# Seven products of half matrices in a float32 output projection on one Trainium2 core

## The chip, the cores and the metric

The kernel runs on one core of one Trainium2 chip. The metric is device time in microseconds (us), as the median of several runs. The engines are named as in the profile: PE is TensorE (matmuls), PEld its weight loads, DVE is VectorE, ACT is ScalarE, POOL is GpSimd, SP is SyncE, which here only issues DMAs. "SP's queue", "ACT's queue" and "POOL's queue" are the DMAs that an engine issues, in its program order: a DMA that has to wait holds up those behind it, and the engine's own work too.

## What is computed

The kernel mixes an attention block A and a block of product-key experts B with a gate per token. S = 2048 tokens, D = 1024, 32 heads of 32.

```python
def _A_ref(x, wqkv, wo):
    ...
    p = _softmax(scores, axis=-1)
    o = jnp.einsum("bhqk,bhkd->bhqd", p, v)
    return (lambda x, *d: x.transpose(*d))(o, 0, 2, 1, 3).reshape(B, S, D) @ wo

def _B_ref(x, w_q, k1, k2, u, v):
    ...
    act = _gelu(jnp.einsum("nd,nhkd->nhk", xf, ue))
    out = jnp.einsum("nhk,nhk,nhkd->nd", g, act, ve)
    return out.reshape(B, S, D)

x = A_x
g = _sigmoid((x * gate_w).sum(-1, keepdims=True))
a = _A_ref(x, A_wqkv, A_wo)
b = _B_ref(x, B_w_q, B_k1, B_k2, B_u, B_v)
return g * a + (1 - g) * b
```

The change concerns the last product, `o @ wo` (2048 x 1024 by 1024 x 1024), and what is added to it from B: a 2048 x 64 matrix of weights (with 1 - g in it) times the 64 x 1024 table v.

## The kernel before

Large products are made in float32r: an operand x is split into hi (x copied to float32r by ACT) and lo (x - hi, by DVE), and hi·hi + hi·lo + lo·hi is summed in PSUM, three matmuls for one. A matmul multiplies 128 x 128 weights into 128 x 512 moving elements, which fill one bank of PSUM. The function `split` (lines 88 to 90) issues one ACT and one DVE instruction.

The order is written out by hand: each engine runs its instructions in the order of the program. The stages, in this order:

- Q and K for all heads, from x and wqkv (line 325); the keys' fold; then the router (line 401 and its helpers).
- The values' stage: V for 16 tiles of 128 tokens, in two halves of 512 columns (`values`, line 566). A tile has 24 matmuls. `values_out` copies a bank to SBUF on ACT (line 569) and stores it by ACT's queue. The banks come from a ring of 8 in the pool `ps1`. The last tile of the second half, tile 15, uses a bank of the pool `pso`, which takes the place of bank 7 when `ps1` is closed; bank 7 was last used by tile 14. Within this stage the experts' weights are turned (`peer_turn`, lines 611 to 620) and stored to DRAM as `ATD`, through a tile `at` with one buffer.
- The 32 heads: scores (line 725), exp on ACT (735), the product with V (746) and sums of rows. `finish` stores a head's unscaled output to DRAM (`OD`); `norm_sums` stores its sums (`SMD`), `load_r` and `norm_r` make reciprocals for four heads and store them (`RD`). Meanwhile wo (`wo_raw`, 16 pieces of 256 KB), v and AT are loaded for the last stage, each at a step of its own.
- The output projection: 8 chunks of 256 tokens (W = 256). A chunk is loaded transposed by `load_chunk(n, k0, k1)` on SP's queue (8 loads of `OD` into a buffer named V, and 4 of the reciprocals, each row to 32 partitions, into rb0 or a buffer named accd), for chunk 1 on POOL's queue. Chunk 0 comes in eighths kc = 0 to 7 as wo is split (`split_hi`, `split_lo`); the last eighth, kc = 7, needs the sums of head 31, made right at the start of this stage: sums to `SMD` (smd<-ssb), back (rr<-smd), reciprocal, to `RD` (rd<-rr), back for each chunk (rb<-rd, accd<-rd). The chunks 1 to 7 are scaled and split by `split_o` one chunk ahead. `wo_mm` makes the 4 banks of a chunk (2 blocks of 128 tokens by 2 halves of 512 columns), 24 matmuls each; `av_mm` adds two matmuls of the experts to each bank. `store` copies a chunk's banks by ACT and DVE in turn and stores them by SP's queue.

Of the kernel before, what the change touches and what calls it, by code (L numbers as in the profile page):

```python
# [9 lines left out]
F32 = mybir.dt.float32  # L10
# [6 lines left out]
S = 2048  # L17
# [13 lines left out]
def gated_mha_peer_kernel(ctx, tc, xT, wqkv, wv, wo, wq, k12, ug, v, out):  # L31
# [537 lines left out]
    def values_out(ts, ps, half, copy=lambda o, p: nc.scalar.activation(o, p, AF.Copy)):  # L569
# [75 lines left out]
    load_shift(0, Z)  # L645
    values_out(*fin0)
    values_out(*values(list(range(4)), 1))
    for t in range(4, NT - 1):
        values_out(*values([t], 1))

    ps1.close()
    pso = Pool("pso", space=PSUM, side="right")

    values_out(*values([NT - 1], 1, lambda: pso.tile([128, 512], F32, name="o")),
               nc.vector.tensor_copy)
    vw.close()
    sm2.close()
    sm.close()
# [3 lines left out]


    keep = Pool("keep")
    wo_raw = keep.tile([128, KC, D], F32, name="wo_raw")
    v_raw = keep.tile([128, D], F32, name="v_raw")
    AT = keep.tile([128, S], F32R, name="AT")
    rb0 = keep.tile([128, KC, W], F32, name="rb0")
    wk = Pool("wk", bufs=2)
    vpool = Pool("vpool", bufs=2)  # L670
    kq = Pool("kq")
# [162 lines left out]
    def split_first(step):  # L834
        o = OC[0][:, 0, :]
        if step == 0:
            W0.append(zp.tile([128, 2, D], F32R, name="z1"))
            OH[0] = zp.tile([128, KC, W], F32R, name="z0")
            OL[0] = wk.tile([128, KC, W], F32R, name="acc")
            nc.vector.tensor_mul(o, o, RB[0][:, 0, :])  # L840
        elif step == 1:
            nc.scalar.activation(W0[0][:, 0], wo_raw[:, 0, :], AF.Copy)
        elif step == 2:
            nc.scalar.activation(OH[0][:, 0, :], o, AF.Copy)
        else:
            for lo, src, hi in ((W0[0][:, 1], wo_raw[:, 0, :], W0[0][:, 0]),
                                (OL[0][:, 0, :], o, OH[0][:, 0, :])):
                nc.vector.tensor_tensor(out=lo, in0=src, in1=hi.bitcast(F32), op=OP.subtract)

# [2 lines left out]
    def at(step, f, *a):  # L852
        todo.setdefault(step, []).append((f, a))
# [16 lines left out]
        at((H - 1) * NT + step, split_first, i)  # L870
    at((H - 1) * NT + 13, merge, H - 1)
    for k in range(2 * KC):
        c = slice(k * D // 2, (k + 1) * D // 2)
        at((8 + k) * NT + 11, dma, wo_raw.rearrange("p k m -> p (k m)")[:, c], wo[:, c])
    for i in range(2):
        at(28 * NT + 6 + i, dma, v_raw[64 * i:64 * i + 64, :], v)
        at(28 * NT + 13 + 10 * i, dma, AT[:, i * S // 2:(i + 1) * S // 2],
           ATD[:, i * S // 2:(i + 1) * S // 2])
# [24 lines left out]
    kq.close()  # L903


    fin = Pool("fin")
    ps_even = Pool("ps_even", space=PSUM)

# [6 lines left out]
    def split_o(n, k0, k1):  # L915

        if k0 == 0:
            OH[n] = zp.tile([128, KC, W], F32R, name=f"z{n % 2}")
            OL[n] = wk.tile([128, KC, W], F32R, name="acc")
        o = OC[n][:, k0:k1, :]  # L920
        nc.vector.tensor_mul(o, o, RB[n][:, k0:k1, :])
        split(OH[n][:, k0:k1, :], OL[n][:, k0:k1, :], o)

    def wo_mm(pa, n, kcs, first, last):
        for kc in kcs:
            wh, wl = (W0[0][:, 0], W0[0][:, 1]) if n == kc == 0 else (woh[kc], wol[kc])
            for a, b, i in ((OH[n], wh, 0), (OH[n], wl, 1), (OL[n], wh, 2)):
                for tt, half in pa:
                    nc.tensor.matmul(pa[tt, half], a[:, kc, tt * 128:(tt + 1) * 128],  # L929
                                     b[:, half * 512:(half + 1) * 512],  # L930
                                     start=(first and kc == kcs[0] and i == 0),
                                     stop=(last and kc == kcs[-1] and i == 2))

    def av_mm(pa, n):
        for (tt, half), ps in pa.items():
            tok = slice(n * W + tt * 128, n * W + (tt + 1) * 128)
            for b in (vh, vl):
                nc.tensor.matmul(ps, AT[:, tok], b[:, half * 512:(half + 1) * 512],  # L938
                                 start=False, stop=False)

    def banks(n):
        pool = (ps_even, ps_odd)[n % 2]
        return {(tt, half): pool.tile([128, 512], F32, name=f"pa{tt}{half}")
                for tt in range(W // 128) for half in range(2)}

    def store(pa, n, pieces=1):
        m = 512 // pieces
        for (tt, half), ps in pa.items():
            r = fin.tile([128, 512], F32, name="res", bufs=3)
            for i in range(pieces):  # L950
                c = slice(i * m, (i + 1) * m)
                if (half + i) % 2:
                    nc.scalar.activation(r[:, c], ps[:, c], AF.Copy)
                else:
                    nc.vector.tensor_copy(r[:, c], ps[:, c])
                dma(out[n * W + tt * 128:n * W + (tt + 1) * 128,
                        half * 512 + i * m:half * 512 + (i + 1) * m], r[:, c])


    def split_hi(kc):  # L960
        nc.scalar.activation(woh[kc], wo_raw[:, kc, :], AF.Copy)
        if kc < KC - 1:
            o = OC[0][:, kc, :]
            nc.vector.tensor_mul(o, o, RB[0][:, kc, :])
            nc.scalar.activation(OH[0][:, kc, :], o, AF.Copy)

    def split_lo(kc):
        nc.vector.tensor_tensor(out=wol[kc], in0=wo_raw[:, kc, :],
                                in1=woh[kc].bitcast(F32), op=OP.subtract)
        if kc < KC - 1:  # L970
            nc.vector.tensor_tensor(out=OL[0][:, kc, :], in0=OC[0][:, kc, :],
                                    in1=OH[0][:, kc, :].bitcast(F32), op=OP.subtract)

    ps_odd = None
    pa = banks(0)
    wo_mm(pa, 0, [0], True, False)
# [3 lines left out]
    load_chunk(1, 0, KC - 1, nc.gpsimd)  # L980
    split_hi(1)
# [12 lines left out]
    split(woh[0], wol[0], wo_raw[:, 0, :])  # L994
    ps_odd = Pool("ps_odd", space=PSUM)
    vhl = fin.tile([128, 2, D], F32R, name="vhl")
    vh, vl = vhl[:, 0], vhl[:, 1]
    split(vh, vl, v_raw)
    av_mm(pa, 0)
    split_lo(KC - 1)  # L1000
    split_o(0, KC - 1, KC)
    wo_mm(pa, 0, [KC - 1], False, True)
    for k0, k1 in ((0, KC // 2), (KC // 2, KC)):
        split_o(1, k0, k1)
    load_chunk(2, 0, KC)
    NW = S // W
    for n in range(NW - 2):
        nxt = banks(n + 1)
        wo_mm(nxt, n + 1, list(range(KC - 1)), True, False)
        av_mm(nxt, n + 1)  # L1010
        split_o(n + 2, 0, KC)
        if n + 3 < NW:
            load_chunk(n + 3, 0, KC)
        store(pa, n)
        wo_mm(nxt, n + 1, [KC - 1], False, True)
        pa = nxt

    n = NW - 1
    for k, (key, ps) in enumerate(banks(n).items()):
        one = {key: ps}  # L1020
        wo_mm(one, n, list(range(KC - 1)), True, False)
        av_mm(one, n)
        if k == 0:
            store(pa, n - 1)
        wo_mm(one, n, [KC - 1], False, True)
        store(one, n, 2)
    ps_odd.close()
    ps_even.close()
    fin.close()
# [32 lines left out]
```

## Time and profile before

| what | us |
|---|---|
| median of 3 runs | 1886.46 (1884.76 to 1887.77) |
| profiled execution, its own time | 1886.32 |
| its span, first to last instruction | 1884.6 |
| matmul of wo, 128x512: busy / weight load | 0.389 / 0.188 |
| copy of a 128x512 bank: ACT / DVE | 0.60 / 0.68 |
| subtraction on DVE: 128x256 / 512 / 1024 / 2048 | 0.42 / 0.69 / 1.22 / 2.29 |
| values' stage, matmuls from 480.7 to 658.1 | 177 |
| heads, from 658.2 to 1688.7 | 1031 |
| output projection, from 1688.7 to the end | 196 |

The span is what the profile's instructions cover; the execution's own time has 1.7 us around it. The granted clock of TensorE is 0.998 on the mean. In the page, a share is of the span. The chain of waits follows the execution back from its last instruction: at each step it goes to what released that instruction, so an engine with a large share there sets the time. In the timelines a line reads: start, length, engine and line of the kernel, operation, out<-in, shapes, and in brackets the idle time before it and what ended it. Matmuls overlap: a busy time of 0.389 us stands for one that starts every 0.227 us. In the values' stage between 480 and 652 us DVE is busy for 32.2 us and ACT for 30.2 us of 172; the DMA engines are used to 24%.

### The profile page before, as it was taken

The numbers are of one execution on the slowest core, as the hardware profiler recorded it, in microseconds if no ns is written. First come the engines' busy times: TensorE is split into PE (matmuls) and PEld (weight loads), VectorE is DVE, ScalarE is ACT, GpSimd is POOL, SyncE is SP. The second block draws the span as 40 slices with busy tenths as digits, with TensorE's granted clock in tenths as the row PEclk, the third lists the DMA queues.
The fourth block names the chain that finished last, engine by engine and source line by source line (L and its number), as shares of the span: only waits on it lengthen the run. The fifth ranks groups of instructions, "written<-read, shape, count | busy, mean of one in ns | idle before, by whom it ended". The sixth has DMA issues, their size and how long they took to land.

```text
span 1884.6 us, 25741 instructions
## 1 busy us (share of the span) xinstructions
PE 1874.6 (99%) x10271; PEld 1157.2 (61%) x10271; DVE 1203.3 (64%) x917; ACT 1158.3 (61%) x1412; POOL 148.6 (8%) x183
## 2 busy tenths in 40 slices
PE   9999999999999999999999999999999999999999
PEld 7877777887888844444444444444444444448887
DVE  4522224877520078888888888888888888895220
ACT  4211111200121199999999999999999999993110
POOL 0000000035200000000000000000000000010000
PEclk9999999999999999999999999999999999999999
DMA  5777774420222177777777777777687777756521
GB/s 212 279 265 254 266 275 137 136 77 5 79 95 80 45 178 159 168 167 162 166 172 179 169 181 169 184 166 181 158 187 162 172 166 177 189 128 167 155 90 67
DMA packets 108082, 302.72 MB, mean 161 GB/s; under 512 B 14724, under 2 KB 48660, under 8 KB 84472
## 3 DMA queue, kind: packets, MB, share of 16 engines
q1 hardware_dynamic: 70520, 154.76, 27.3%
q0 software_dynamic: 14976, 103.29, 26.4%
q10 hardware_dynamic: 22464, 43.00, 7.1%
q8 instruction: 81, 1.33, 0.3%
q14 instruction: 41, 0.34, 0.1%
HBM read 138.73 MB, written 62.66 MB: 107 GB/s over the span
## 4 chain that ended last, share of the span: by engine, by line
PE 99%; ACT 0%; DMA 0%; DVE 0%; issue 0%; ACTq 0%; DVEq 0%
PE ring L725 28%; PE o L746 25%; PE bk L325 16%; PE pa L929 9%; PE bk L566 9%; PE bk L401 5%; PE bk L211 2%; PE bk L272 2%; PE ring L759 1%; PE pa L938 1%; PE o L566 0%; DMA w0raw<-in_wqkv 0%; PE bk L286 0%; PE o L759 0%; ACT P L735 0%
## 5 line engine op out<-in xcount | busy, mean ns | idle before, releaser
L735 ACT ACTIVATE P<-ring 128x512 f32<-128x512 f32 (+2 forms) x1034 | 914.5, 984 | 22.2 <-PE ring L725 8.2
L774 DVE TENSOR_TENSOR acc<-acc,P 128x2048 f32<-128x2048 f32 x319 | 731.0, 2291 | 76.3 <-ACT P L735 50.0
L746 PE MATMUL o<-P,V 128*32 128x512 f32 x3840 | 465.4, 599 | 0.0
L725 PE MATMUL ring<-z,z 98*128 98x512 f32 x1024 | 273.0, 408 | 1.4 <-ACT P L735 1.1
L725 PE MATMUL ring<-Q,K 98*128 98x512 f32 x1024 | 272.0, 407 | 0.2 <-ACT P L735 0.2
L725 PEld LDWEIGHTS ring<-z,z 98*128 98x128 f32 x1024 | 182.6, 188 | 144.4 <-ACT P L735 75.4
L725 PEld LDWEIGHTS ring<-Q,K 98*128 98x128 f32 x1024 | 182.0, 188 | 144.3 <-ACT P L735 72.7
L746 PEld LDWEIGHTS o<-P,V 128*32 128x32 f32 x3840 | 98.8, 109 | 223.5 <-issue 214.7
L89 ACT ACTIVATE hi<-bk 128x512 fp32r<-128x512 f32 x64 | 37.6, 598 | 242.8 <-PE bk L325 226.4
L325 PE MATMUL bk<-xh,whi 128*128 128x512 f32 x448 | 176.2, 393 | 0.1
L325 PE MATMUL bk<-xh,wlo 128*128 128x512 f32 x448 | 174.4, 389 | 0.0
L325 PE MATMUL bk<-xl,whi 128*128 128x512 f32 x448 | 174.4, 389 | 0.0
L768 POOL DMA_DIRECT2D accd<-P x95 | 81.5, 858 | 1100.4 <-ACT P L735 368.6
L90 DVE TENSOR_TENSOR lo<-bk,hi 128x512 fp32r<-128x512 f32 x64 | 44.2, 690 | 188.1 <-ACT hi L89 183.9
L772 DVE TENSOR_TENSOR acc<-P 128x2048 f32<-128x2048 f32 x32 | 73.4, 2292 | 74.3 <-ACT P L735 74.3
L325 PEld LDWEIGHTS bk<-xh,whi 128*128 128x128 f32 x448 | 84.1, 188 | 24.0 <-issue 6.7
L566 PE MATMUL bk<-wvh,xh 128*128 128x512 f32 x248 | 96.7, 390 | 0.0
L566 PE MATMUL bk<-wvh,xl 128*128 128x512 f32 x248 | 96.5, 389 | 0.0
L566 PE MATMUL bk<-wvl,xh 128*128 128x512 f32 x248 | 96.5, 389 | 0.0
L325 PEld LDWEIGHTS bk<-xh,wlo 128*128 128x128 f32 x448 | 84.1, 188 | 17.8
L325 PEld LDWEIGHTS bk<-xl,whi 128*128 128x128 f32 x448 | 84.1, 188 | 17.0
L569 ACT ACTIVATE vo<-bk 128x512 f32<-128x512 f32 x31 | 18.5, 597 | 109.3 <-PE bk L566 103.4
(163 smaller groups left out, 1660.7 us busy)
## 6 DMA issues: line engine op xcount, KB each, us to landing
accd<-P POOLq DMA_DIRECT2D x95, 1024.0 KB, 7.5
wqt<-in_wq SPq DMA_DIRECT2D x32, 1024.0 KB
vd<-vo ACTq DMA_DIRECT2D x32, 256.0 KB
z<-kdh SPq DMA_DIRECT2D x32, 256.0 KB
z<-qdh SPq DMA_DIRECT2D x32, 256.0 KB
V<-vd SPq DMA_DIRECT2D x32, 256.0 KB
K<-kdh SPq DMA_DIRECT2D x32, 256.0 KB
Q<-qdh SPq DMA_DIRECT2D x32, 256.0 KB
```

Source lines behind the costliest of these rows:

```text
L90: (on or nc.vector).tensor_tensor(out=lo, in0=src, in1=hi.bitcast(F32), op=OP.subtract)
L211: nc.tensor.matmul(b0[w, n], w0[w][a][:, kc, :], b[:, kc, n * 512:(n + 1) * 512], start=(kc == 0 and i == 0), stop=(kc == KC - 1 and i == 2))
L325: nc.tensor.matmul(ps, a[:, kc, :], b[:, kc, n * 512:(n + 1) * 512], start=first, stop=last)
L401: nc.tensor.matmul(ps, a[:, kc, tok], b, start=first, stop=last)
L566: nc.tensor.matmul(p, a[:, kc, tok], b, start=first, stop=last)
L725: on_ring(nc.tensor.matmul(ring[:, i, :], K[:98, kt * 128:(kt + 1) * 128], Q[:98, qc * 512:(qc + 1) * 512], start=True, stop=True), i)
L735: on_ring(nc.scalar.activation(P[h, kt][:, q0 * 512:(q0 + m) * 512].rearrange("p (a m) -> p a m", a=m), ring[:, i:i + m, :], AF.Exp, scale ...
L746: nc.tensor.matmul(O[h][32 * qc:32 * qc + 32, :], Vt[g][:, kt, 32 * j:32 * j + 32], p[:, qc * 512:(qc + 1) * 512], start=(kt == 0), stop=( ...
L768: nc.gpsimd.dma_start(ACCD[h], P[h, kt], accum_op=OP.add)
L772: nc.vector.tensor_add(ACC[h], P[h, 0], P[h, kt])
L774: nc.vector.tensor_add(ACC[h], ACC[h], P[h, kt])
L929: nc.tensor.matmul(pa[tt, half], a[:, kc, tt * 128:(tt + 1) * 128], b[:, half * 512:(half + 1) * 512], start=(first and kc == kcs[0] and i ...
```

## The change

A product of 2 x 2 half matrices can be made with seven products of halves (in the Winograd form) in place of eight. For the chunks 1 to 7, A is the chunk's 256 tokens x 1024 and B is wo; A11 is the first 128 tokens by the first 512 of the inner dimension, A12 those tokens by the other 512, and B11 the first 512 rows by the first 512 columns. The combinations are S1 = A21 + A22, S2 = S1 - A11, S3 = A11 - A21, S4 = A12 - S2 and T1 = B12 - B11, T2 = B22 - T1, T3 = B22 - B12, T4 = B21 - T2, and each product is split into hi and lo as before. A chunk is one `unit`: the products A11·B11, S3·T3, S1·T1, S2·T2, A12·B21, S4·B22, A22·T4 (12 matmuls each), the experts' matmuls (two for each of the four results, one result in a bank of its own), and sums of the banks on DVE. In a unit the next chunk is scaled, combined and split (`ahead`); the places of the operands have one buffer each, freed by the product that reads them. Chunk 0 is made as before, but the first product of chunk 1 is put ahead of its last eighth.

The combinations T1 to T4 don't depend on the chunk. They are made in the values' stage, in four groups i = 0 to 3 (`load_early`, `split_early`), and stored to DRAM (`TD`); a fifth group does v (`VPD`). The loads of group i stand behind `values_out` of tile 4 + 2i, the subtractions and splits behind that of tile 5 + 2i. In the last stage `load_t` loads them (2 loads of 1 MB each for T1 to T3, 8 of 256 KB for T4), partly over buffers of wo that are done with. AT is loaded by chunk. `norm_r` and the loads of the last eighth move from inside the loop over kc to behind it.

The core of the diff:

```diff
+    TD = [[dram.tile([128, KC // 2, 512], F32R, name=f"t{i}{part}") for part in "hl"] for i in range(4)]
+    VPD = [dram.tile([128, D], F32R, name=f"vp{part}") for part in "hl"]
...
     values_out(*values(list(range(4)), 1))
+    th = Pool("th", bufs=2)
+    raw = {}
+
+    def load_early(i):
+        for j in range(4 if i < KC // 2 else 2):
+            raw[j] = wvp.tile([128, 512], F32, name="wvraw")
+            if i < KC // 2:
+                c0 = (i + j // 2 * KC // 2) * D + j % 2 * 512
+                dma(raw[j], wo[:, c0:c0 + 512])
+            else:
+                for k in range(2):
+                    dma(raw[j][64 * k:64 * k + 64, :], v[:, j * 512:(j + 1) * 512])
+
+    def split_early(i):
...
+        def parts(t, dst_hi, dst_lo):
+            hi, lo = th.tile([128, 512], F32R, name="th"), t.bitcast(F32R)
+            split(hi, lo, t)
+            dma(dst_hi, hi)
+            dma(dst_lo, lo)
+
+        if i < KC // 2:
+            b11, b12, b21, b22 = (raw[j] for j in range(4))
+            sub(b11, b12, b11)
+            sub(b12, b22, b12)
+            sub(b22, b22, b11)
+            sub(b21, b21, b22)
+            for k, t in enumerate((b11, b22, b12, b21)):
+                parts(t, *(d[:, i, :] for d in TD[k]))
+        else:
+            for j in range(2):
+                parts(raw[j], *(d[:, j * 512:(j + 1) * 512] for d in VPD))
+
     for t in range(4, NT - 1):
         values_out(*values([t], 1))
+        (load_early, split_early)[t % 2](t // 2 - 2) if t < NT - 2 else None
...
+    def product(a, b, *av):
+        ps = bank()
+        if av:
+            av_mm(*av, ps, first=True)
+        for k in range(HC):
+            for i, j in ((0, 0), (0, 1), (1, 0)):
+                nc.tensor.matmul(ps, AP[a][i][:, k, :], BP[b][j][k],
+                                 start=(not av and k == 0 and i == j == 0),
+                                 stop=(k == HC - 1 and i == 1))
+        return ps
...
     load_chunk(1, 0, KC - 1, nc.gpsimd)
+    for n in range(2):
+        load_at(n)
+    load_t(2, [zp.tile([128, S], F32R, name="z1")], [fin.tile([128, S], F32R, name="t3l")])
...
         if kc == 4:
-            norm_r(G - 1)
-            for n in range(2):
-                load_chunk(n, KC - 1, KC)
-        wo_mm(pa, 0, [kc], False, False)
+            load_t(0, *([keep.tile([128, S], F32R, name=f"wo_raw{i}")] for i in range(2)))
+        wo_mm(pa, [kc], False, False)
+    norm_r(G - 1)
+    for n in range(2):
+        load_chunk(n, KC - 1, KC)
+    split_lo(KC - 1)
+    split(woh[0], wol[0], raw_wo(0))
+    load_t(1, *([keep.tile([128, S], F32R, name=f"wo_raw{i}")] for i in range(2, 4)))
...
+    scale_o(1, 0)
+    operand(1, "A11")
...
+    p1 = product("A11", "B11")
+    o = OC[0][:, KC - 1, :]
+    nc.vector.tensor_mul(o, o, RB[0][:, KC - 1, :])
+    split(OH[0][:, KC - 1, :], OL[0][:, KC - 1, :], o)
+    wo_mm(pa, [KC - 1], False, True)
+    operand(1, "S3")
+    scale_o(1, 1)
+    operand(1, "S1")
     load_chunk(2, 0, KC)
+    load_at(2)
+    load_t(3, *([part[k][:, 512:] for k in range(HC)] for part in (woh, wol)))
...
+        p7 = product("S3", "T3")
...
+        p5 = product("S1", "T1")
...
+        p6 = product("S2", "T2")
+        tt(u2, c1, p6)
+        tt(u3, u2, p7)
+        tt(u2, u2, p5)
+        tt(u5, u3, p5)
...
+            p2 = product("A12", "B21", n, 0, 0)
...
+            p3 = product("S4", "B22", n, 0, 1)
...
+            av_mm(n, 1, 1, ps, True, True)
...
+            p4 = product("A22", "T4", n, 1, 0)
...
+    for n in range(1, S // W):
+        unit(n, p1 if n == 1 else product("A11", "B11"))
```

In the code the raw tiles hold the lo parts after the split (`lo` is `t` itself), and in the last unit the first result, c11, is made last and stored in two pieces.

More of the change, by code (lines that the diff above doesn't have):

```diff
@@ L913, in gated_mha_peer_kernel, with load_at, wo_mm @@
             parts[kc] = fin.tile([128, D], F32R, name=f"wo{'hl'[parts is wol]}{kc}")
[L915 to L924, printed above, removed]
+    HC = KC // 2
+    AT = {}
+    def load_at(n):
+        AT[n] = fin.tile([128, W], F32R, name="at", bufs=3)
+        dma(AT[n], ATD[:, n * W:(n + 1) * W])
+    def wo_mm(pa, kcs, first, last):
         for kc in kcs:
[L926 to L927 removed]
+            wh, wl = (W0[0][:, 0], W0[0][:, 1]) if kc == 0 else (woh[kc], wol[kc])
+            for a, b, i in ((OH[0], wh, 0), (OH[0], wl, 1), (OL[0], wh, 2)):
                 for tt, half in pa:
@@ L932, in wo_mm, with av_mm, bank, store @@
                                      stop=(last and kc == kcs[-1] and i == 2))
[L934 to L957, printed above, removed]
+    def av_mm(n, tt, half, ps, first=False, last=False):
+        for i in range(2):
+            nc.tensor.matmul(ps, AT[n][:, tt * 128:(tt + 1) * 128],
+                             vhl[:, i, half * 512:(half + 1) * 512],
+                             start=(first and i == 0), stop=(last and i == 1))
+    bank_no = [0]
+    def bank():
+        i = bank_no[0] % 8
+        bank_no[0] += 1
+        return (ps_even, ps_odd)[i // 4].tile([128, 512], F32, name=f"pa{i}")
+    def store(n, tt, half, r, c=slice(0, 512)):
+        dma(out[n * W + tt * 128:n * W + (tt + 1) * 128, half * 512 + c.start:half * 512 + c.stop],
+            r[:, c])
     def split_hi(kc):
-        nc.scalar.activation(woh[kc], wo_raw[:, kc, :], AF.Copy)
+        nc.scalar.activation(woh[kc], raw_wo(kc), AF.Copy)
         if kc < KC - 1:
@@ new lines, in gated_mha_peer_kernel, with osb, unit, ahead @@
+    post = rb0.rearrange("p k m -> p (k m)").rearrange("p (a m) -> p a m", m=512)
+    def osb():
+        return wk.tile([128, 512], F32, name="osb")
+    ORDER = ("A11", "S3", "S1", "S2", "A12", "S4", "A22")
+    def unit(n, p1):
+        u2, u3, u5 = (post[:, i] for i in range(3))
+        last = n == S // W - 1
+        def ahead(*names):
+            if last:
+                return
+            for name in names:
+                if name == "A11":
+                    scale_o(n + 1, 0)
+                    scale_o(n + 1, 1)
+                operand(n + 1, name)
+        c1 = osb()
+        nc.scalar.activation(c1, p1, AF.Copy)
+        if n == 1:
+            for (i, half), ps in pa.items():
+                r = osb() if i == half == 0 else post[:, 2 * i + half]
+                if half:
+                    nc.scalar.activation(r, ps, AF.Copy)
+                else:
+                    nc.vector.tensor_copy(r, ps)
+                store(0, i, half, r)
+            for name in ("S2", "A12", "S4", "A22"):
+                operand(n, name)
+        if n + 2 < S // W:
+            load_chunk(n + 2, 0, KC)
+            load_at(n + 2)
+        if n > 1:
+            ahead("A11")
+        p7 = product("S3", "T3")
+        if n > 1:
+            ahead("S3")
+        p5 = product("S1", "T1")
+        if n > 1:
+            ahead("S1")
+        p6 = product("S2", "T2")
[3 more added lines that the diff above has]
+        tt(u5, u3, p5)
+        if n > 1:
+            ahead("S2")
+        def c11():
+            p2 = product("A12", "B21", n, 0, 0)
+            pieces = 2 if last else 1
+            for i in range(pieces):
+                c = slice(i * 512 // pieces, (i + 1) * 512 // pieces)
+                tt(c1[:, c], c1[:, c], p2[:, c])
+                store(n, 0, 0, c1, c)
+        def c12():
+            p3 = product("S4", "B22", n, 0, 1)
+            tt(u2, u2, p3)
+            store(n, 0, 1, u2)
+        def c22():
+            ps = bank()
+            av_mm(n, 1, 1, ps, True, True)
+            tt(u5, u5, ps)
+            store(n, 1, 1, u5)
+        def c21():
+            p4 = product("A22", "T4", n, 1, 0)
+            tt(u3, u3, p4)
+            store(n, 1, 0, u3)
+        if not last:
+            c11()
+            ahead(*((() if n > 1 else ORDER[:4]) + ("A12",)))
+        c12()
+        ahead("S4")
+        c22()
+        c21()
+        ahead("A22")
+        if last:
+            c11()
```

102 lines of the change are left out of this document (59 added, 43 removed).

## The prediction

> **What bounds the kernel now.** I read the page's busy times and its chain first, then the chain piece by piece, then the timelines of ACT, SP and PE around the two stages that the change touches, and last stretches of clock and DMA. The page's first line and its chain say that TensorE sets the time:
>
> ```profile
> PE 1874.6 (99%) x10271; PEld 1157.2 (61%) x10271; DVE 1203.3 (64%) x917; ACT 1158.3 (61%) x1412; POOL 148.6 (8%) x183
> ...
> PE 99%; ACT 0%; DMA 0%; DVE 0%; issue 0%; ACTq 0%; DVEq 0%
> ```
>
> In the last stage the chain in order of time (start, us, what) is one unbroken row of matmuls:
>
> ```profile
> 1712.76 21.76 PE pa L929 x96
> 1736.33 21.76 PE pa L929 x96
> 1759.90 21.76 PE pa L929 x96
> ```
>
> A piece is 96 matmuls in 21.76 us, 0.2267 us each, and the next starts 23.57 us later: 104 x 0.2267 (96 of wo, 8 of v). Every matmul that goes is worth 0.2267 us there, and every wait that PE gets is paid in full.
>
> In the values' stage PE works without a gap too, but its last tile has a wait. ACT's timeline (start, us, engine, line) shows the copy of a tile whose successors matter below and the last copy from ring bank 7; PE's shows the first matmul into the bank that replaces it:
>
> ```profile
> 603.00 0.60 ACT L569 ACTIVATE vo<-bk 128x512 f32<-128x512 f32 x1 [4.84 <-PE bk L566]
> ...
> 651.96 0.60 ACT L569 ACTIVATE vo<-bk 128x512 f32<-128x512 f32 x1 [4.84 <-PE bk L566]
> ```
> ```profile
> 652.61 0.50 PE L566 MATMUL o<-wvh,xh 128*128 128x512 f32 x1 [0.69 <-ACT vo L569]
> ```
>
> Tile 15 of the second half can't start before ACT has copied tile 14, and all that stands ahead of this copy in ACT's order can delay it. The copies before it have eight banks, so ACT may be late there without PE noticing. The 32 heads follow with PE busy 99%: what is lost here is not won back.
>
> **1. Fewer matmuls.** A unit has 7 products of 4 x 3 matmuls and 8 of v: 92 in place of 104. Seven chunks: 84 x 0.2267 = **-19.0 us**. The operands keep their shapes; a weight load takes 0.188 us, below the pitch. In a steady unit DVE has, by the nearest rows, two scalings of 128x1024 (1.22 each) and 19 sums and splits of 128x512 (0.69 each): 15.5 us of 20.9; ACT has 8 copies, 4.9. Every operand is made a unit ahead of its product and each of the eight banks is used once a unit, so PE covers them; what it costs if DVE is slower than these rows is rival (c). The loads of AT by chunk (128 KB) hide likewise behind a chunk's 2 MB, which arrive a unit early. The end (two pieces of 0.42 on DVE, before one of 0.38 on ACT and one of 0.42) is even, -0.3 to +0.3.
>
> **2. The combinations in the values' stage.** Added: 16 loads of wo (256 KB), 4 of v (128 KB), 36 stores (256 KB), all on SP's queue, which issues nothing else from 567 to 658; 16 subtractions and 18 lo on DVE (23.5 us, idle there) and 18 hi on ACT (11.3). By busy time it is nothing; the order decides. Each hi has one of two buffers in `th` (lo stays in the raw tile), so a hi waits until the hi two before it has been stored. What a store takes, one buffer's chain shows:
>
> ```profile
> 548.07 0.60 ACT L619 ACTIVATE at<-bk 128x512 fp32r<-128x512 f32 x1 [2.26 <-DMA atd<-at]
> 550.91 0.60 ACT L619 ACTIVATE at<-bk 128x512 fp32r<-128x512 f32 x1 [2.24 <-DMA atd<-at]
> ```
>
> 2.1 to 2.2 us after its issue the buffer is free. The first split comes behind tile 5's copy and its DMA, at 604.0 us, with data long there: hi at 604.0, 604.6, 606.8 (the first one's store), 608.2, the last lo until 609.6. SP then loads the next group, each tile as its lo has been stored, the last issue at 612.2; 2.5 later four subtractions of 0.69 run. The next group's hi stands behind tile 7's copy anyway, at 614.8, PE's pace of 10.9 us for two tiles. Such a later group lasts longer: its first lo waits for all four subtractions (2.0 to 3.5 after hi 0), and the stores behind that lo in SP's queue slip with it, so it takes 11.3 to 12. The groups start at 614.8, 626.1, 638.2, v's at 648.9 (no subtractions), and v's second hi ends at 650.3. Tile 14's copy is due at 651.96: **0 us**, by a slack of 1.7. From above: with stores of 2.8 in place of 2.14, or transfers a third slower, each group takes 1.5 to 2.5 more and the copy comes 6 to 10 late; behind it wait tile 15, V's loads on SP and the scores. DMA is the cover here: a group moves 12 x 262 KB and its two tiles 2 more, 3.7 MB in 10.9 us, 337 GB/s; such rows ran at 262 GB/s at 70% of the engines, so 374 when full:
>
> ```profile
> 552.00:554.00 2.00, 2.00 (x10) 1.66 (x9) 0.69 (x1) 0.63 (x1) 0.00 (x0) 1.00 0.70 262
> ```
>
> By the Trainium skill (DMA: Bandwidth & Descriptors, Bandwidth) a 1 MB transfer reaches 341 GB/s, which would leave the groups no slack at all. This trace has 430 and more for 8 KB rows (step 3), so I keep the rows; the warning is in the bound.
>
> **3. Into the last stage.** T1 to T3 are 2 x 1 MB each, T4 8 x 256 KB, on SP's queue among the chunks and the last head's sums; the reciprocals (norm_r) and the loads of eighth 7 go behind the loop over wo's eighths. POOL's queue keeps chunk 1 alone. Stretches (busy of each engine, clock, DMA share, GB/s): 8 KB rows at 430 GB/s, and the engines full just where the sums' 8 KB pass:
>
> ```profile
> 20.00:22.00 2.00, 2.00 (x11) 1.65 (x10) 0.50 (x1) 0.43 (x1) 0.00 (x0) 1.00 1.03 432
> ...
> 1694.00:1696.00 2.00, 2.00 (x11) 1.42 (x8) 2.00 (x5) 1.55 (x3) 0.87 (x2) 1.00 1.01 301
> 1696.00:1698.00 2.00, 2.00 (x10) 1.64 (x9) 2.00 (x5) 2.00 (x4) 0.65 (x2) 1.00 0.95 132
> ```
> ```profile
> 1695.07 0.48 SPq L71 DMA_DIRECT2D smd<-ssb  x1
> 1701.72 0.34 SPq L71 DMA_DIRECT2D rr<-smd  x1
> 1704.32 0.34 SPq L71 DMA_DIRECT2D rd<-rr  x1
> ```
>
> The sums, issued at 1695.07, let SP go on at 1701.7, when chunk 1's loads on POOL's queue end. T3's 2.1 MB (4.9 us at 430) now stand ahead of them: 1706.5. To the reciprocal 1.8, through it 0.8: 1709.2, and DVE, which waits there, has the rest of wo's splits behind it. The reciprocals' store stands behind T1: 4.9 + 1.4 first, landed at 1713.8; rb's reads 1.7 + 1.5, scaling and hi 0.42 each: chunk 0's last eighth starts at 1718.1. PE would be there at 1712.6 + 2.7 (the first product, put ahead of it), 1715.3: **2.8 us**. A PE that has waited then runs slowly:
>
> ```profile
> 663.00:666.50 3.50, 3.50 (x13) 1.66 (x17) 1.32 (x1) 3.50 (x5) 0.00 (x0) 0.51 1.13 287
> ```
>
> In PE's timeline three waits of 0.23, 0.84 and 0.38 us between 660 and 663 came before these 3.5 us at half clock; so 3.4 x 0.5 = **1.7**. The Trainium skill (TensorE: Matmul & The Clock Gate, Part 1: The HAM clock gate) has the clock halved after an idle window of about 3.4 us; by that 2.8 us would cost no clock, and the sum would be 1.7 lower. Here 1.45 us of waits were enough.
> T2 (issued 1718.5, landed 1724.8) is due at 1718.1 + 3 x 2.72 = 1726.3: hidden, by 1.5. T4 stands behind chunk 2, whose 2.1 MB need 9.8 us at the 215 GB/s that DMA moved from 1714 to 1726: 1734.6; its own 2.1 MB at 374: 1740.2. The last matmuls of its product are due at 1738.3, with the slow clock 1739: **1.5**. Together **6.0**. From below 0: DMA was used to 9-41% from 1702 to 1712, and if small transfers pass between large ones all fits. From above 14: T3, T1 and T4 late by 4 to 5 each.
>
> **Sum.** -19.0 + 0 + 6.0 = -13.0 on the profiled execution's 1886.32 (span 1884.6, 1.7 around it; the runs' median is 1886.46, 0.14 above): 1873.3, rounded up for step 2's one-sided bound to **1874 us**.
>
> **Rivals.**
> (a) *All of it hides.* -19.0: 1867, at best 1866.7. For it: the low DMA share from 1702 to 1712. Against: full engines from 1694 to 1700, where the chain of the sums starts, and no slack in it before (last scaling 1710.9, its matmuls 1712.6).
> (b) *A cover tears: groups of splits slower than PE's pace, or T loads and chunks colliding.* Step 2 at 6 to 10, or step 3 at 14: 1879 to 1884. For it: 337 of 374 GB/s in the one, 13 MB from 1690 to 1740 (270 GB/s) in the other.
> (c) *VectorE becomes the bound of the units; slower.* Its operands are now read in runs of 128 elements out of 256, and sums mix PSUM and SBUF. From 1.07 us for a 128x512 on, its 19 of them and 2.44 of scaling take 22.7 us a unit and the gain is gone (7 x 1.85); at 1.25 it is 26.2, +37 on the forecast: 1911. For it: eq<-eq,mm (128x512, one source repeated along its rows) takes 0.92. Against: a split into runs of 64 (z<-z, line 90) takes 1.22 for 1024 like a plain one, and eq<-bk,m from PSUM 0.62 for 448.
> That the matmuls don't go is no case: the loops count them; the page would show 10187 on PE.
>
> **Chances.** Forecast 0.46, (a) 0.20, (b) 0.24, (c) 0.10. A measurement of this kernel can't tell less than about 0.2%, 3.8 us, from no change. Faster: the forecast, (a) and most of (b), 0.84; same: (b)'s end and the mild (c), 0.07; slower 0.09. Range: from (a), 1866.5, to (b)'s end with a little of both its halves, 1885.
>
> **What would show it.** Right: units 20.9 us apart; ACT's hi waiting for stores two before, v's second hi ended before 652, tile 14's copy at 652; PE waiting for chunk 0's last eighth near 1715 and for T4 near 1736, clock 0.5 between. Wrong: tile 14's copy near 660 and PE idle there; units longer than 20.9 with PE waiting for DVE; PE unbroken from 1688 on (then 1867); a longer tail.

## The result and the profile after

| | before | after |
|---|---|---|
| median of 6 runs each, us | 1885.61 (1884.06 to 1887.77) | 1893.93 (1892.16 to 1895.43) |
| profiled execution / its span, us | 1886.32 / 1884.6 | 1892.16 / 1890.4 |
| first score of the heads, us from the start | 658.19 | 667.52 |
| last stage begins / lasts, us | 1688.66 / 195.9 | 1696.38 / 194.0 |

The ratio is 1.0042 [1.0029, 1.0055]: slower by 0.4%, where 13 us less were forecast. The span grew by 5.8 us. The table's last two lines split this: everything ahead of the last stage became 7.7 us longer, and the last stage, which lost 84 matmuls or 19.0 us, only 1.9 shorter: 17.1 were given back. The 7.7 have luck in them: the first score of the heads came 9.3 later, and the heads themselves took 1.6 less (1028.9 us, 1030.5 before) because the slow clock at their start, 0.51 in the profiled execution before, was 1.00 in this one (last section). The first lines of the page and its chain by engine:

```profile
PE 1860.9 (98%) x10187; PEld 1143.2 (60%) x10187; DVE 1285.2 (68%) x1066; ACT 1179.9 (62%) x1461; POOL 148.8 (8%) x183
...
PE 93%; DMA 4%; DVE 1%; ACT 1%; SPq 0%; issue 0%; ACTq 0%; DVEq 0%
```

The 84 matmuls went, and PE fell from 99% of the chain to 93%; DMA has 4% where it had none. The steady units are as forecast. The chain in order of time (start, us, what) has them 20.86 us apart, 92 x 0.2267, with nothing but PE in it:

```profile
1779.38 13.60 PE pa L1070 x60
...
1800.24 13.60 PE pa L1070 x60
...
1821.09 13.60 PE pa L1070 x60
```

So the loss lies where the unit isn't steady yet. The list of PE's waits (us in total, times, longest) names the places:

```profile
PE o L569 <- ACT vo L572: 9.1, 1, 9.1
PE pa L1070 <- ACT acc L92: 7.8, 2, 5.1
PE pa L980 <- ACT z L92: 2.6, 1, 2.6
...
PE pa L1070 <- DMA wol<-t3l: 0.7, 1, 0.7
```

**The values' stage.** ACT's timeline shows the first hi of the groups 1, 2, 3 and of v, and the copy of tile 14 (due at 651.96):

```profile
616.79 0.63 ACT L92 ACTIVATE th<-wvraw 128x512 fp32r<-128x512 f32 x1 [2.71 <-DVE wvraw L669]
...
631.40 0.63 ACT L92 ACTIVATE th<-wvraw 128x512 fp32r<-128x512 f32 x1 [5.52 <-DVE wvraw L669]
...
646.12 0.63 ACT L92 ACTIVATE th<-wvraw 128x512 fp32r<-128x512 f32 x1 [5.78 <-DVE wvraw L669]
...
658.49 0.63 ACT L92 ACTIVATE th<-wvraw 128x512 fp32r<-128x512 f32 x1 [4.05 <-DMA wvraw<-in_v]
...
659.96 0.58 ACT L572 ACTIVATE vo<-bk 128x512 f32<-128x512 f32 x1
```

The groups came 13.2 (from 603.6), 14.6, 14.7 and 12.4 us after one another, not 10.8 to 12. The brackets tell why: ACT stood 2.7 to 5.8 us for DVE's subtraction, which waited for the group's loads. The chain within the first two groups shows what a transfer took in company (in the lines t0 to t3 in DRAM are T1 to T4, h and l their hi and lo):

```profile
605.41 3.97 DMA t1h<-th
...
610.85 3.56 DMA t3l<-wvraw
...
614.47 3.38 DMA wvraw<-in_wo
...
621.13 2.54 DMA t1h<-th
...
625.14 3.45 DMA t3l<-wvraw
...
628.61 3.27 DMA wvraw<-in_wo
```

On this chain a store of a hi, priced at 2.14 from a lone one, took 3.97 us in the first group and 2.4 to 3.0 in the later ones; a store of a lo took 3.4 to 3.6 in the first three groups, and a load 3.3 to 3.4 in place of 2.5. They stand in series: a load waits for the store that empties its tile. So tile 14's copy came at 659.96, 8.0 late, and PE's timeline has the wait, 0.69 before:

```profile
660.59 0.80 PE L569 MATMUL o<-wvh,xh 128*128 128x512 f32 x1 [9.06 <-ACT vo L572]
```

Behind it the granted clock was 0.50 until 663.4, which cost 1.35 us more.

**The last stage.** PE's timeline has the four waits, 11.1 us together:

```profile
1723.21 0.50 PE L1070 MATMUL pa<-woh,acc 128*128 128x512 f32 x1 [2.73 <-ACT acc L92]
...
1729.11 2.07 PE L980 MATMUL pa<-woh,z 128*128 128x512 f32 x4 [2.61 <-ACT z L92]
...
1751.35 0.50 PE L1070 MATMUL pa<-wol,acc 128*128 128x512 f32 x1 [0.66 <-DMA wol<-t3l]
...
1759.29 0.80 PE L1070 MATMUL pa<-woh,acc 128*128 128x512 f32 x1 [5.12 <-ACT acc L92]
```

The first is chunk 1's first product, the second chunk 0's last eighth, the third T4, the fourth the first product of chunk 2, which the prediction doesn't mention. Matmuls at half clock behind them cost some 5.4 us (the 12 from 1729.11 take 5.28, not 2.72); the remaining 0.6 is spread. The chain from the last head's sums on:

```profile
1702.80 13.81 DMA smd<-ssb
1716.63 1.63 DMA rr<-smd
...
1719.12 5.49 DMA rd<-rr
...
1725.97 1.99 DMA rb<-rd
```

The store of the sums, 8 KB, took 13.81 us behind T3's 2 MB on SP's queue (6.6 before), and that of the reciprocals 5.5 behind T1's (1.5). The fourth wait's cause is in the timelines of DVE and of SP's queue:

```profile
1754.84 2.01 DVE L1039 TENSOR_TENSOR rb<-rb,pa 128x512 f32<-128x512 f32 x3 [10.91 <-DMA out<-rb]
...
1757.36 2.35 DVE L1046 TENSOR_TENSOR V<-V,accd 128x1024 f32<-128x1024 f32 x2
```
```profile
1740.52 4.49 SPq L74 DMA_DIRECT2D woh<-t3h  x4
1745.06 3.59 SPq L74 DMA_DIRECT2D wol<-t3l  x4
...
1749.47 1.88 SPq L74 DMA_DIRECT2D out<-rb  x3
```

Chunk 0's results are staged in rb0. The unit's sum u3 writes there too, so DVE waits until they're stored, and their stores stand behind T4's eight loads, each of which took SP about 1 us to issue (4.49 and 3.59 for four). These loads didn't wait for their places, halves of wo's rows, which were last written by a split of DVE that ended at 1721.4 and which only chunk 0 had read; they stood behind chunk 2's, which SP issued from 1729.8 on. DVE did nothing for 10.9 us, then scaled chunk 2, and PE waited for its first operand.

### The profile page after: what moved, and what is told of

It reads as the page before. It is cut to its first block, busy times and chain, and to the rows that moved or that the text cites. A ratio compares the mean times of both kernels' runs of the same rounds, so it can differ in the third digit from the quotient of the medians.

```text
span 1890.4 us, 25992 instructions
## 1 busy us (share of the span) xinstructions
PE 1860.9 (98%) x10187; PEld 1143.2 (60%) x10187; DVE 1285.2 (68%) x1066; ACT 1179.9 (62%) x1461; POOL 148.8 (8%) x183
## 4 chain that ended last, share of the span: by engine, by line
PE 93%; DMA 4%; DVE 1%; ACT 1%; SPq 0%; issue 0%; ACTq 0%; DVEq 0%
PE ring L773 28%; PE o L794 25%; PE bk L328 16%; PE pa L1070 7%; PE bk L569 6%; PE bk L404 5%; PE bk L214 2%; PE bk L275 2%; PE ring L807 1%; DMA smd<-ssb 1%; DMA t1h<-th 1%; PE pa L987 1%; DMA t3l<-wvraw 1%; DMA wvraw<-in_wo 1%; PE pa L980 0%; SPq L74 0%
## 5 line engine op out<-in xcount | busy, mean ns | idle before, releaser
L328 PEld LDWEIGHTS bk<-xh,wlo 128*128 128x128 f32 x448 | 84.1, 188 | 17.7
L1070 PE MATMUL pa<-woh,acc 128*128 128x512 f32 x224 | 74.4, 397 | 7.8 <-ACT acc L92 7.8
```

Of the source, the lines that this page charges most:

```text
L328: nc.tensor.matmul(ps, a[:, kc, :], b[:, kc, n * 512:(n + 1) * 512], start=first, stop=last)
L1070: nc.tensor.matmul(ps, AP[a][i][:, k, :], BP[b][j][k], start=(not av and k == 0 and i == j == 0), stop=(k == HC - 1 and i == 1))
```

## Experiments

Ratios are to the kernel before, run beside each on the same chip; a difference from the changed kernel is one of ratios (0.1% is 1.9 us).

### The groups begun earlier

```diff
+    load_early(0)
+    split_early(0)
+    load_early(1)
     values_out(*values(list(range(4)), 1))
+    split_early(1)
+    load_early(2)
...
         values_out(*values([t], 1))
-        (load_early, split_early)[t % 2](t // 2 - 2) if t < NT - 2 else None
+        if t in (5, 8, 10):
+            i = {5: 2, 8: 3, 10: 4}[t]
+            split_early(i)
+            if i < 4:
+                load_early(i + 1)
```

> The same groups of wo's combinations, begun behind the last tiles of the first half in place of tile 5, so some 20 us earlier; nothing else differs from the changed kernel. Theory (the loss in the values' stage is ACT's order: groups of 14.4 us end too late for tile 14's copy): PE's wait of 9.1 us ahead of tile 15 falls to 0.7, tile 14's copy is at 652 again, and the time falls by some 7 to 8 us from the changed kernel's, to about 1886. Rival (the DMA of the groups itself slows the stage, or what is saved is paid again at the heads' start): the wait moves into another tile or to the first scores, and the time stays at 1892 to 1894.

Median 1883.63, ratio 0.9993 [0.9983, 1.0002]: 0.49% less than the changed kernel, 9 us. PE's timeline has tile 15's wait back at its old length:

```profile
652.36 0.50 PE L569 MATMUL o<-wvh,xh 128*128 128x512 f32 x1 [0.69 <-ACT vo L572]
```

The last stage began at 1688.18, as before the change. The groups themselves were no faster, the last three 13.3 to 14.6 us after one another; they only had more time. The loss in the values' stage is thus wholly one of when, and is settled.

### Chunk 0's stores on POOL's queue

```diff
-            r[:, c])
+            r[:, c], nc.gpsimd if n == 0 else nc.sync)
```

> Chunk 0's four stores are issued on POOL's queue in place of SP's, where they stood behind T4's eight loads. Theory (the wait of 5.1 us ahead of chunk 2's first product is DVE, held by the sum that overwrites chunk 0's results in rb0 until they are stored): DVE's idle time of 10.9 us ends near 1745, the wait of 5.1 us and the slow clock after it go, and the time falls by 6 to 7 us, to about 1887. Rival (chunk 2's own loads come that late): DVE then waits for chunk 2 in place of the stores, and PE's wait stays above 4 us.

Median 1889.7, ratio 1.0022 [1.0012, 1.0033]: 3.8 us less than the changed kernel. The wait of 5.12 is gone, but T4's grew, in the timelines of PE and of SP's queue:

```profile
1752.09 0.47 PE L1070 MATMUL pa<-woh,acc 128*128 128x512 f32 x1 [2.22 <-DMA woh<-t3h]
...
1754.57 0.79 PE L1070 MATMUL pa<-wol,acc 128*128 128x512 f32 x1 [2.01 <-DMA wol<-t3l]
```
```profile
1742.21 5.47 SPq L74 DMA_DIRECT2D woh<-t3h  x4
1747.73 4.35 SPq L74 DMA_DIRECT2D wol<-t3l  x4
```

The mechanism is confirmed: a wait for a buffer that is freed by a store behind other transfers. DVE made the sum u3 at 1743.4, not 1754.8, and then stood 4.9 us for chunk 2's reciprocals, so the rival had a part in it too. What it gave fell short of 6 to 7 because T4's product stands ahead of chunk 2's in PE's order, and T4's loads now came later: they were issued 1.7 and 2.7 us behind the changed kernel's, with chunk 0's stores, 1 MB, now moving ahead of them.

### The two small stores on ACT's queue

```diff
-        dma(SMD[g][j:j + 1, :].rearrange("o (q s) -> (o q) s", q=NQ), o[::32, :])
+        dma(SMD[g][j:j + 1, :].rearrange("o (q s) -> (o q) s", q=NQ), o[::32, :],
+            nc.scalar if h == H - 1 else nc.sync)
...
-        dma(RD[g].rearrange("j (b m) -> (j b) m", m=64), r)
+        dma(RD[g].rearrange("j (b m) -> (j b) m", m=64), r, nc.scalar if g == G - 1 else nc.sync)
```

> The last head's sums (8 KB) and its reciprocals (32 KB) are stored from ACT's queue in place of SP's, so that T3's and T1's loads no longer stand ahead of them in the same queue; the loads themselves are as they were. Theory 1 (the small transfers wait in their queue's order): the sums are back some 6 us earlier (SP waits 7 us for them, not 14), the reciprocals' store takes 1.5 us in place of 5.5, PE's two waits of 2.7 and 2.6 us and the slow clock after them go, -7 to -9 us. Theory 2 (the 16 DMA engines are full, and any small transfer waits for what is ahead on the engines, whichever queue it came by): the sums land within 2 us of where they did, and the time moves by less than 3 us.

Median 1895.94, ratio 1.0060 [1.0042, 1.0077]: not faster, and 3 us slower if anything. The chain shows both halves of the answer:

```profile
1702.60 6.95 DMA smd<-ssb
...
1709.57 10.77 DMA rr<-smd
```

The store was quick again (6.95, from 13.81), so its place in the queue was what held it. But the read behind it, still on SP's queue, took 10.77 in place of 1.63: 17.7 for both, 15.4 in the changed kernel.

### The three together

The earlier groups, chunk 0's stores on POOL's queue and the small stores on ACT's, in one kernel.

> All three edits together. If the three causes are separate and each theory holds, the savings add: -7 to -8, -6 to -7 and -7 to -9, so about 1871 to 1874, below the kernel before. If the last stage is bound by the bytes it moves (T's 8 MB, chunks and stores by 1760), the second and third edit together save no more than one of them, and it stays above 1877.

Median 1877.92, ratio 0.9961 [0.9947, 0.9975]: faster than before by 0.4%, 15 us less than the changed kernel, yet above 1877, where it was expected to stay if bytes bound the last stage. 4.64 us of wait for the first product stayed (7.14 + 9.76 for sums and read), and 2.87 + 1.96 for T4. Of the gain on before, 1.9 us are luck in the profiled execution's clock at the heads' start (last section).

### The read of the sums moved too

```diff
-        dma(R[g], SMD[g].rearrange("j (b m) -> (j b) m", m=64))
+        dma(R[g], SMD[g].rearrange("j (b m) -> (j b) m", m=64), nc.gpsimd if g == G - 1 else nc.sync)
```

> As e3, and the read of the last head's sums (rr<-smd, 32 KB) goes by POOL's queue, where e3 left it on SP's behind T3: there the sums landed after 6.9 us (1709.6) but the read took 10.8 more. Theory 1 (a small transfer waits for what stands ahead of it in its own queue): the read takes 2 to 3 us, the reciprocal comes at about 1713 in place of 1720.4 (1718.3 in the changed kernel), PE's wait ahead of the first product falls from 5.5 to below 1 us, and the time is some 5 us below e3's and 3 below the changed kernel's, about 1890. Theory 2 (full engines hold any queue): the reciprocal stays behind 1717.

On top of the two small stores on ACT's queue. Median 1892.6, ratio 1.0035 [1.0023, 1.0048]. The read was issued on POOL's queue, where nothing but chunk 1's loads had been, and DVE had it 10.9 us later:

```profile
1722.15 0.55 DVE L855 RECIPROCAL rr<-rr 128x64 f32<-128x64 f32 x1 [9.09 <-DMA rr<-smd]
```

So order within a queue isn't the whole of it: SP, no longer held by the sums, issued T1's 2 MB at 1704.9 and 1709.5, and the same engines then served these and the read. By the Trainium skill (DMA: Bandwidth & Descriptors, Issuing engines are not separate DMA queues) the DMAs of all issuing engines interleave on the same 16 engines, and starting them from several saves only the time to start them. The reads of 10.8 and 10.9 us from either queue agree with that; the store that went from 13.81 to 6.95 shows that the place behind 2 MB in one queue counted too. Why that store then passed T3's 2 MB and the read did not, the runs don't show.

### Four buffers for hi

```diff
-    th = Pool("th", bufs=2)
+    th = Pool("th", bufs=4)
```

> The changed kernel with four buffers in th in place of two, so that no hi waits for a store of its own group. Theory (a group of 14.4 us is a row of waits for transfers that take 3.4 to 4.0 us in each other's company, not 2.14): hi 2 and hi 3 come 2 us earlier, a group falls to about 12, PE's wait of 9.1 us ahead of tile 15 to about 1 to 3. Rival (the DMA engines move a group's 3.7 MB no faster): groups stay above 14 and the wait above 8.

A single execution: 1891.29, last stage at 1695.43. ACT's timeline has the group of 644.5 with three hi at once, and the wait ahead of its first longer than ever:

```profile
644.50 0.63 ACT L92 ACTIVATE th<-wvraw 128x512 fp32r<-128x512 f32 x1 [8.16 <-DVE wvraw L669]
646.86 1.67 ACT L92 ACTIVATE th<-wvraw 128x512 fp32r<-128x512 f32 x3 [1.72 <-DVE wvraw L669]
```

The buffers of hi, which the prediction worked its groups from, weren't the main limit: the groups stood 11.8 to 14.9 apart and tile 15 waited 7.77. What is left is the round of store, load and subtraction on the four raw tiles.

### A better order in the last stage

```diff
+    split_lo(KC - 1)
+    split(woh[0], wol[0], raw_wo(0))
+    scale_o(1, 0)
+    operand(1, "A11")
     norm_r(G - 1)
...
+    operand(1, "S3")
     p1 = product("A11", "B11")
+    p7 = product("S3", "T3")
     o = OC[0][:, KC - 1, :]
```

The first four lines and S3 move ahead from further down, and S3·T3 is made before chunk 0's last eighth. This on top of the three together, with the read on POOL's queue:

> e4's three edits, the read of the sums by POOL's queue, and an order in which DVE finishes wo's splits and the first product's operand ahead of the reciprocal, and PE makes the second product (S3 by T3) ahead of chunk 0's last eighth too. If PE's waits at the start of the last stage are the sums' round trip alone, they are covered: no wait ahead of the first product, below 1 us ahead of the last eighth, and e4's 1877.9 falls by 5 to 7 us, to about 1872. The waits for T4 (4.9 us in e4) stay, since T4 stands behind chunk 2 as before; if they grow by what the others lose, the stage is bound by its bytes and the time stays at 1876 to 1878.

Median 1882.79, ratio 0.9982 [0.9972, 0.9992]: a clear miss, 4 us worse than the three without it. By the profiled executions the last stage is 2.8 us longer (192.9, 190.1); it also began 2.4 later, mostly by the heads' clock. DVE's timeline shows the new wait, for chunk 1's scales on POOL's queue:

```profile
1713.36 1.23 DVE L1054 TENSOR_TENSOR V<-V,accd 128x1024 f32<-128x1024 f32 x1 [7.45 <-DMA accd<-rd]
```

With T1 issued earlier, chunk 1's loads became the late ones. The same order with the small transfers left on SP's queue:

> e7 with the small transfers left on SP's queue as in the changed kernel: the groups begun early, chunk 0's stores on POOL's queue, and the new order alone. If order covers the round trip by itself, within 1 us of e7; if the queue matters, PE waits 3 to 5 us ahead of chunk 0's last eighth and the time is 1875 to 1878.

Median 1882.58, ratio 0.9980 [0.9969, 0.9992], waits of 3.00 (last eighth), 3.27 and 1.95 (T4). The time is equal to the one before it, as expected if order alone covered the sums' round trip, but the wait of 3.00 shows that it didn't. With chunk 0's stores moved (alone, with the three together, and here twice), PE waits 8.2 to 9.6 us in the last stage in all four arrangements: who is served first mostly decides who waits.

### T not loaded at all

```diff
-                dma(place, src[:, m * j:m * j + m, :].rearrange("p k m -> p (k m)"))
+                nc.gpsimd.memset(place.bitcast(F32), 0.05)
```

With the earlier groups; everything else of the last stage is as in the change.

> As e1 (groups begun early), with the loads of T1 to T4 left out: GpSimd writes a constant in their places, so the products with T hold wrong numbers; the time of PE's work is the same. Theory (what is lost in the last stage is the 8 MB of T among the chunks on the same DMA engines): e1's waits there (3.0, 1.6, 1.2, 2.0, 3.1 us, and the slow clock after them) fall to below 2 us in all, and the time falls from 1883.6 to 1867 to 1869, which is the whole gain of the matmuls. Rival (the order: the first product and norm_r's new place behind wo's splits, chunk 0's stores): without T's bytes more than 4 us of waits stay, and it is above 1873.

Median 1866.69, ratio 0.9900 [0.9884, 0.9917]. PE's list of waits has no line for the last stage at all; its one line from near the change is

```profile
PE o L569 <- ACT vo L572: 0.7, 1, 0.7
```

The stage took 176.7 us, 195.9 - 19.2. The sums' store took 7.8 and the read 1.6, both on SP's queue. Two stretches (length, busy of PE, PEld, DVE, ACT and POOL, clock, DMA share, GB/s) begin within 0.3 us of the first matmul of A22·T4 (1750.3 and 1731.0), in the changed kernel and then without T's loads:

```profile
1750.00:1760.00 10.00, 4.22 (x17) 2.63 (x15) 5.13 (x7) 0.63 (x1) 0.00 (x0) 0.96 0.95 311
```
```profile
1731.00:1741.00 10.00, 10.00 (x46) 8.29 (x45) 6.88 (x12) 3.61 (x7) 0.00 (x0) 1.00 0.49 142
```

DMA is at 0.95 with PE at 42% in the one, at 0.49 with PE at 100% in the other. PE's last wait for T4 ended at 1751.35 and its last part was in use at 1753.6: what fills the engines behind it are chunk 0's stores and chunk 3's loads, issued from 1748.8 on, behind T4's in SP's queue. The whole loss of the last stage, late sums, late chunks, the overwritten rb0 and T4, thus comes of T's loads. The products, sums and splits of the new scheme are covered. This run takes T's 8 MB from the engines and T's places from SP's queue at once, so by itself it doesn't tell bytes from places.

### Half the bytes

T is stored unsplit and split again in the last stage, by ACT and DVE, in the place of its lo: 4 MB to store and 4 to load, not 8 and 8. The order is the better one for wo's splits and the first operand, the groups are where the change put them.

```diff
-                parts(t, *(d[:, i, :] for d in TD[k]))
+                dma(TD[k][:, i, :], t)
...
+    def split_t(i):
+        for hi, lo in TP[i]:
+            split(hi, lo, lo.bitcast(F32))
```

> The combinations T1 to T4 are stored unsplit (4 MB in place of 8) and split into hi and lo in the last stage, in the places where they are loaded; the groups stay where the change put them, and the last splits of wo and the first product's operand go ahead of the reciprocal on DVE. Theory (both losses are bytes): a group moves 2.1 MB and two tiles' 0.5 and has no hi on ACT, so it takes below 10.9 us and tile 14's copy is at 652, no wait at tile 15; in the last stage half of T's bytes go, the waits fall to 3 to 6 us in all: 1870 to 1875. Rival (DVE, which gets 9.6 us of splits more in the first 40 us of the stage, becomes what PE waits for): the waits for ACT and DVE grow there as those for DMA shrink, 1876 to 1882.

Median 1874.45, ratio 0.9935 [0.9919, 0.9952], within what was expected: 0.65% below before, 1.1% below the change. Without splits in the groups ACT has nothing to do there, DVE's subtractions ran from 576 to 617, and tile 15 waited its old 0.69; so in the values' stage this run doesn't tell fewer bytes from a free ACT. The last stage took 187.4; its waits, in PE's timeline:

```profile
1715.27 1.63 PE L980 MATMUL pa<-woh,z 128*128 128x512 f32 x4 [2.11 <-ACT z L92]
...
1727.14 3.31 PE L1077 MATMUL pa<-wo_raw,z 128*128 128x512 f32 x12 [1.80 <-ACT z L92]
...
1742.07 0.50 PE L1077 MATMUL pa<-woh,acc 128*128 128x512 f32 x1 [1.38 <-ACT acc L92]
```

With chunk 0's stores on POOL's queue as well:

> As e10, with chunk 0's stores on POOL's queue as in e2. If the sum that overwrites chunk 0's results still waits for their stores behind T4 in e10, PE's wait ahead of chunk 2's first product goes and this is 2 to 5 us below e10; if half of T's bytes have cleared the queue by then, the two are equal within 1 us.

Median 1872.72, ratio 0.9935 [0.9918, 0.9951]: the same. Its longest wait, 3.27, is for S2, which stands behind T2's split on DVE; with S2 combined ahead of that split:

> As e11, and chunk 1's S2 is combined ahead of T2's split and split right behind it, ahead of the copies of chunk 0's banks. In e11 PE waits 3.3 us for S2's hi at the product S2 by T2, with a slow clock after it (1.4). If that operand is what the product waits for, the wait falls below 1.5 us and the time by 2 to 4 us, to about 1869 to 1871. If T2's own split (its lo ends at 1723.0, the product is due at 1722.4) is the limit, the wait stays above 2 us and the time is e11's.

Median 1873.3, ratio 0.9930 [0.9916, 0.9943]. That wait went, and 2.40 for the last eighth, 1.08 for T4's lo and 1.37 for chunk 2 came; the three can't be told apart. All beat both kernels.

## Why the prediction was wrong

The forecast was 1874 in a range of 1866.5 to 1885; 1893.93 lies above it and on the other side of before. By its steps:

- **Step 1, -19.0: right.** 10187 matmuls, units of 20.86 us, no wait for DVE in them (busy 16.9 of 20.9; 15.5 were forecast), so rival (c) fell; the end is even. Without T's loads the stage shrank by 19.2.
- **Step 2, 0: wrong, 9.3** (7.7 with the heads' luck). The mechanism was named, in (b) and as what would show it wrong: tile 14's copy near 660 (659.96) and PE idle there. The size that failed was that of a transfer: 2.14 us for a store and 2.5 for a load, taken from lone ones, in a step that itself worked out 337 GB/s of an assumed 374. The first store was still as priced (the third hi came at 606.47, 606.8 forecast); from then on the stores and loads of the chain took 2.4 to 4.0, and a group 12.4 to 14.7, not 11.3 to 12. The mean use of DMA didn't show it: 0.66 from 600 to 652. Within a group the engines were full for one part and far from it for another, while DVE subtracted and split:

```profile
616.00:622.00 6.00, 6.00 (x28) 4.98 (x27) 4.55 (x7) 1.90 (x3) 0.00 (x0) 1.00 0.37 137
622.00:630.00 8.00, 8.00 (x37) 6.64 (x36) 0.81 (x2) 1.72 (x3) 0.00 (x0) 1.00 0.96 349
```

  So a group takes its transfers at full engines and then the work on DVE and ACT, one after the other; the cover that the step counted on was not there. The rate wasn't what failed: these 349 at 0.96 of the engines scale to 364, between the 374 that I scaled from a stretch at 70% and the 341 GB/s of the Trainium skill (DMA: Bandwidth & Descriptors, Bandwidth). The two buffers of hi, on which the working was built, weren't the main limit. Given the measured transfers, "6 to 10 late" for stores of 2.8 was about right; the chosen value was not.
- **Step 3, +6.0: wrong, 17.1.** Its terms: for the sums' chain 2.8 of waits were forecast and 5.3 measured (2.73 + 2.61); for the slow clock behind them 1.7, and some 3.6; for T4 1.5, and 0.7. The sums' store was priced 4.9 later behind T3, a transfer alone at 430 GB/s; it was 7.2 later. The largest term, 6.9 (5.12 and 1.8 of clock), is not in the working: rb0 holds chunk 0's results when the first unit's sums want it, and their stores had been put behind T4's loads. The prediction followed the loads through SP's queue, but not the stores. Two of its sums are off by little: the reciprocals' store, from the figures beside it, lands up to 1 us earlier than 1713.8, and T4's 1740.2 less 1739 is 1.2, not 1.5.
- **The two covers were one.** Rival (b) had "step 2 at 6 to 10, or step 3 at 14", one or the other. Both tore, step 3 by more, and in the main for one reason: T goes out and comes in through engines already used, and the stores and loads of T and the sums' store behind T3 were priced as if each had the engines to itself. Had both ends been added, 8 and 14 to -19, the sum would have been +3, near the 5.8 measured.

T's loads left out show that these loads are the cause of the last stage's loss. That their bytes are, more than their places, is argued from two things: moving single transfers to other queues mostly changed who bore it, and half the bytes took the stage from 194.0 to 187.4 and 182.9. These runs also changed the order of splits, and T's loads at another time, during the heads, weren't tried. What stays open, too, is why half the bytes still cost some 6 to 11 us of the stage (182.9 to 187.4 against 176.7): splits now stand in ACT's and DVE's order too, and they weren't tried without the loads.

## What to carry to other kernels

Price a transfer by a row in which the engines are as full as they will be, and a chain of load, compute and store over the same buffers as the sum of its parts, not by mean use. When work is hidden under a busy engine at both ends of a round trip through DRAM, the two covers share one resource, so their bad ends belong in one case; here fewer bytes helped more than moving them between queues. When loads go into a queue, list the stores behind them, and ask which buffer each of them frees.

## What the runs showed of the hardware

The same three waits of PE (0.23, 0.84 and 0.38 us, within 0.01) stand at the heads' start, between 659.3 and 662.9, in the kernel before, in the one with earlier groups and in seven later ones. The stretch behind them without T's loads:

```profile
663.00:666.50 3.50, 3.50 (x24) 1.50 (x23) 2.05 (x1) 3.50 (x5) 0.00 (x0) 1.00 1.07 262
```

The clock there is 1.00, and so it is in five others. It was 0.51 in the profiled execution before (shown in the prediction), 0.60 with earlier groups and 0.53 in the first kernel with the better order. The heads took 1030.2 to 1030.5 us in these three and 1028.5 to 1028.8 in the six: equal waits cost 1.6 us or nothing. Their time from the start doesn't decide it: in the two kernels with the better order they end at 662.8, and the clock behind is 0.53 in one and 1.00 in the other. The 52 runs of the kernel before beside the experiments may show the same: 22 with a mean clock of 1.000 took 1883.6 to 1885.8 us, 19 at 0.998 took 1885.9 to 1888.2, and the other 11 lie across both. The Trainium skill (TensorE: Matmul & The Clock Gate, Part 1: The HAM clock gate) has a free-running window of 3.4 us, by which a run's phase would decide. That agrees, as does the idle of PE from 651.5 in the changed kernel, at which the clock fell only 5.2 us later; but the page has it fall after an idle window, and here it fell behind 1.45 us of waits within some 3 us.
